# The second half of the first layer's w_in tiles serves two token groups at once

## The chip, the cores and the metric

The kernel runs on one core of one Trainium2 chip. The time is device microseconds (us) of one execution; of the kernel before three runs are known. About 0.5% is what a measurement of this kernel can tell from no change.

## The reference

Causal attention in blocks of 64 over 4 batches, 8 heads and 576 positions with 64 elements per head, then two feed-forward layers over all 2304 tokens, in float32:

```
scores = scale * q @ k.T; scores = where(block_i >= block_j, scores, -1e9)
x = softmax(scores) @ v                      # 2304 x 512 after the transpose of the heads
h = x @ w_in; x = (h - tanh(h)) @ w_out      # 512 -> 2048 -> 512
xn = x / sqrt(mean(x*x) + 1e-6) * rms_g
out = (silu(xn @ w_gate) * (xn @ w_val)) @ w_out2   # 512 -> 1536 -> 512
```

The change concerns the first feed-forward layer and the attention that is computed beside it.

## The kernel before

Every matrix product of the layers is made of three TensorE products: a float32 value is split into a rounded part (`h`, by the helper `rnd`, L88, mostly on ScalarE) and the rest (`l`, by `lo`, L94, a subtraction on VectorE or GpSimd), and the product is h*h + h*l + l*h. The page of the profile puts all of these splits down to L90 and L95.

The 2304 tokens are worked on in six groups of 384 (`NG`). The first layer has 16 tile steps (`J1`) in each group. A step `s` = (group g, tile j) has an in-product, L703 to L705 (12 matmuls 128x384, w_in tile j, into a PSUM tile `t`), then tanh on ScalarE (L711), `h - tanh(h)` on VectorE (L712, the kernel's "gelu" results), the split into `gh` and `gl`, and, one step later, the out-product of that tile, L619 to L621 (9 matmuls 128x512, w_out tile j, into three accumulators `acc`).

The weights of the first layer have to be brought into split form once. `stage1` loads a tile of 512 KB into `st` (L114), `convert` (L117 to L132) makes of it an h half and an l half with three ScalarE and four VectorE instructions (tiles `cv`, `cu`, `w1s`), and L584 writes the result to the DRAM tiles `w1d`. There are 32 tiles, w_in and w_out in turn. Seven of them (`EARLY`) are converted in the stretch before the first step, while the attention of group 0 runs; the other 25 during the 16 steps of group 0, which uses each as it is ready. Groups 1 to 5 load the tiles again from `w1d` (L590, 512 KB each, four buffers each of `w1s0` for w_in and `w1s1` for w_out).

Attention is cut into small steps (scores, transposes, product with v) in one list (`Attn.seq`), and TensorE's program order is written out by hand: `aslot` is called four times in a tile step and puts in as many attention steps as `upto` finds due. `goal(g)` says how far the list has to be by the end of group g: in group 0 to the end of group 1's attention (`end[1]`), in groups 1 to 4 a quarter of the rest each, and never less than the next group needs. Groups 0 and 1 have a lighter form of attention (plain float32, no split, scaling of the probabilities on GpSimd at L472). Group 5 has no attention beside it; there the second layer's weights are converted instead. The second layer (L782 to L822) follows. The order on VectorE, ScalarE, GpSimd and the SP queue is made by a scheduler; all DMAs are issued from SP.

Of the kernel before, what the change touches and what calls it, by code (L numbers as in the profile page):

```python
# [81 lines left out]
def build(ctx, tc, q, k, v, w_in, w_out, w_gate, w_val, w_out2, rms_g, ident_in, mask_in, out):  # L82
# [247 lines left out]
    class Attn:  # L330
# [222 lines left out]
    with tc.manual_schedule(engines={PE.engine}):  # L553
# [12 lines left out]
        for n in range(8):  # L566
            PE.matmul(warm, lhsT=zero[:, 0:128], rhs=zero[:, 0:512], start=True, stop=True)
        staged = {}
# [6 lines left out]
        w1t = {}  # L575

        def w1tile(n):
            return ring.tile([128, 1024], F32R, name=f"w1s{n % 2}", tag=f"w1s{n % 2}")

        def convert1(n):  # L580
# [4 lines left out]
            w1t[n] = (h, l)  # L585

        def w1load(n):
            t = w1tile(n)
            m = n % (2 * J1)
            SP.dma_start(out=t.bitcast(F32), in_=w1d[m])  # L590
            w1t[n] = (t[:, 0:512], t[:, 512:1024])
# [3 lines left out]
        def conv_upto(m):  # L595
            nonlocal ncv
            while ncv < min(m, 2 * J1):
                convert1(ncv)
                ncv += 1
                stage1(ncv + 2)  # L600
# [9 lines left out]

# [12 lines left out]
        def out1(s, t):  # L623
            g, j = divmod(s, J1)
            if j == 0:
                accs[t] = accp.tile([128, DM], F32, name=f"acc{t}", tag=f"acc{t}")
            gh, gl = gts[s]
            wh, wl = w1t[2 * s + 1]
            gemm_out(accs[t], gh, gl, wh, wl, t, j == 0, j == J1 - 1)
            if j == J1 - 1:  # L630
# [39 lines left out]

        NSA = NG * J1
        conv_upto(max(EARLY, 2))
        w2a = None
        nld = 2 * J1
        for s in range(NSA):
            g, j = divmod(s, J1)
            if j == 0:
                if g == 1:
                    st1.__exit__(None, None, None)
                    x4 = tc.tile_pool(name="x4", bufs=1, side="right")  # L680
                    env["x4"] = x4.__enter__()
                base, goal = att.pos, att.goal(g)
                nslots = 4 * J1 - 3
                si = 0

            def aslot():
                nonlocal si
                si += 1
# [157 lines left out]
```

## Time and profile before

| | us |
|---|---|
| median of three runs (lowest, highest) | 1127.95 (1122.27, 1128.41) |
| the profiled execution | 1128.99 |
| its span, first to last instruction | 1127.1 |
| start stretch, up to the first in-product | 57.5 |
| group 0 (16 steps) | 115.3 |
| group 1 | 103.9 |
| groups 2, 3, 4 | 102.6, 103.6, 101.9 |
| group 5 and the second layer | 542.3 |

The stretches are bounded by the first in-product of each group (57.5, 172.8, 276.7, 379.3, 482.9 and 584.8 us). Group 0 is also cut at the start of its tile 8 (109.6 us), and group 1 at its own (226.7 us). Matmuls are pipelined, so that two stand in the record at the same time and a busy TensorE is not TensorE at its peak; what a step really takes is read from the distance of its starts.

### The profile page before, as it was taken

To read this page: it belongs to the slowest core of one execution; us is meant where nothing else is said; L and a number is where in the kernel's file an instruction comes from. 1 tells how busy PE (TensorE), PEld (TensorE's weight loads), DVE (VectorE), ACT (ScalarE), POOL (GpSimd) and SP (SyncE) were. 2 spreads that over 40 slices of the span, in tenths; PEclk is the share of its full clock that TensorE was granted. 3 is DMA by queue.
4 is the path that set the end of the run, shared out by engine and by line. 5 is a ranking of instruction groups with operands and counts; after the bars stand their busy time and mean duration, and the time that the engine had idled before them with its cause. 6 is when DMAs were issued, how large, how long until landed. Compare 5 with 4: busy or idle time off the path is not lost.

```text
span 1127.1 us, 17140 instructions
## 1 busy us (share of the span) xinstructions
PE 1089.7 (97%) x5852; PEld 956.5 (85%) x5852; DVE 689.7 (61%) x1536; ACT 580.8 (52%) x1351; POOL 205.1 (18%) x286
## 2 busy tenths in 40 slices
PE   9899889999999999999999999899999999999998
PEld 6477668888888888788888989799999999999997
DVE  6789887887888878888757878822222222222212
ACT  6677777766777676666656686611112211121111
POOL 2534421343334242424210000000000000000000
PEclk9899999999999999999999999999999999999999
DMA  7799889778988887787569955400000000000000
GB/s 177 210 274 281 263 274 301 199 207 214 236 215 211 235 224 204 190 236 197 182 196 395 363 165 170 140 29 19 10 28 19 30 19 19 29 10 1 29 1 29
DMA packets 215496, 175.64 MB, mean 156 GB/s; under 512 B 159472, under 2 KB 180208, under 8 KB 215408
## 3 DMA queue, kind: packets, MB, share of 16 engines
q1 hardware_dynamic: 215408, 174.54, 53.8%
q8 instruction: 47, 0.77, 0.3%
q14 instruction: 41, 0.34, 0.1%
HBM read 148.28 MB, written 26.21 MB: 155 GB/s over the span
## 4 chain that ended last, share of the span: by engine, by line
PE 62%; DVE 12%; DMA 11%; ACT 7%; issue 3%; SPq 1%; POOL 1%; DVEq 0%; ACTq 0%; POOLq 0%
PE gv L798 8%; PE gv L796 8%; PE gv L797 7%; PE acc L619 7%; PE acc L621 7%; PE acc L620 7%; PE t L703 4%; DMA st<-in_moe_w_out 3%; PE t L705 3%; PE t L704 3%; PE t L436 3%; PE t L488 2%; DMA st<-in_moe_w_val 2%; DVE pt L472 2%; DVE pt L455 2%
## 5 line engine op out<-in xcount | busy, mean ns | idle before, releaser
L796 PE MATMUL gv<-xh,w_h 128*128 128x384 f32 x576 | 195.3, 339 | 2.6 <-ACT w_h L90 2.6
L798 PE MATMUL gv<-xh,w_l 128*128 128x384 f32 x576 | 194.2, 337 | 1.2 <-DVE w_l L95 1.0
L797 PE MATMUL gv<-xl,w_h 128*128 128x384 f32 x576 | 193.4, 336 | 0.0
L806 DVE TENSOR_TENSOR gt<-gv,gt 128x384 f32<-128x384 f32 x72 | 40.0, 556 | 236.0 <-PE gv L798 236.0
L90 ACT ACTIVATE gh<-gt 128x384 fp32r<-128x384 f32 x168 | 87.5, 521 | 152.5 <-DVE gt L806 137.1
L703 PE MATMUL t<-xh,w1s 128*128 128x384 f32 x384 | 140.7, 366 | 7.0 <-ACT w1s L90 5.7
L705 PE MATMUL t<-xh,w1s 128*128 128x384 f32 x384 | 131.2, 342 | 2.5 <-DVE w1s L95 2.4
L458 ACT ACTIVATE pt<-pt,stat 128x128 f32<-128x128 f32 (+3 forms) x160 | 96.1, 601 | 72.2 <-DVE pt L455 70.9
L704 PE MATMUL t<-xl,w1s 128*128 128x384 f32 x384 | 130.3, 339 | 0.0
L619 PE MATMUL acc<-w1s,gh 128*128 128x512 f32 x288 | 123.5, 429 | 3.3 <-ACT x2s L90 1.7
L805 ACT ACTIVATE gt<-gv 128x384 f32<-128x384 f32 x72 | 35.3, 490 | 162.5 <-PE gv L798 162.5
L95 DVE TENSOR_TENSOR gl<-gt,gh 128x384 fp32r<-128x384 f32 x152 | 92.0, 605 | 43.4 <-ACT gh L90 42.9
L621 PE MATMUL acc<-w1s,gl 128*128 128x512 f32 x288 | 114.9, 399 | 3.1 <-POOL gl L95 3.0
L796 PEld LDWEIGHTS gv<-xh,w_h 128*128 128x128 f32 x576 | 108.5, 188 | 6.5 <-ACT w_h L90 4.1
L620 PE MATMUL acc<-w1s,gh 128*128 128x512 f32 x288 | 113.8, 395 | 0.0
L798 PEld LDWEIGHTS gv<-xh,w_l 128*128 128x128 f32 x576 | 108.5, 188 | 2.5 <-DVE w_l L95 2.5
L797 PEld LDWEIGHTS gv<-xl,w_h 128*128 128x128 f32 x576 | 108.6, 189 | 2.4
L621 PE MATMUL acc<-w_h,gl 128*128 128x512 f32 x216 | 85.6, 396 | 0.6 <-DVE gl L95 0.6
L455 DVE TENSOR_SCALAR_CACHE_REDUCE pt<-t 128x128 f32<-128x128 f32 (+3 forms) x160 | 75.6, 473 | 16.4 <-PE t L439 11.1
L620 PE MATMUL acc<-w_l,gh 128*128 128x512 f32 x216 | 85.4, 395 | 0.0
L619 PE MATMUL acc<-w_h,gh 128*128 128x512 f32 x216 | 84.3, 390 | 0.4 <-ACT gh L90 0.4
L703 PEld LDWEIGHTS t<-xh,w1s 128*128 128x128 f32 x384 | 73.4, 191 | 12.2 <-ACT w1s L90 6.6
(101 smaller groups left out, 2140.7 us busy)
## 6 DMA issues: line engine op xcount, KB each, us to landing
w1s<-w1d SPq DMA_DIRECT2D x160, 512.0 KB, 4.6
w1d<-w1s SPq DMA_DIRECT2D x32, 512.0 KB, 5.3
st<-in_moe_w_out SPq DMA_DIRECT2D x28, 512.0 KB, 5.0
st<-in_moe_w_in SPq DMA_DIRECT2D x16, 512.0 KB, 5.3
st<-in_moe_w_gate SPq DMA_DIRECT2D x12, 512.0 KB, 3.9
st<-in_moe_w_val SPq DMA_DIRECT2D x12, 512.0 KB, 5.0
kr<-in_k SPq DMA_DIRECT2D x64, 72.0 KB, 4.2
x2d<-x2s SPq DMA_DIRECT2D x18, 256.0 KB, 3.7
```

Of the source, the lines that this page charges most:

```text
L95: eng.tensor_tensor(out=o, in0=full, in1=hi.bitcast(F32), op=ALU.subtract)
L455: DVE.tensor_scalar(pt[p0:128, a:z], s[p0:128, 0:z - a], -0.125, least, ALU.mult, ALU.min, accum_out=mx[n])
L458: ACT.activation(out=pt[p0:128, 0:keys], in_=pt[p0:128, 0:keys], func=AF.Exp, scale=-1.0, bias=least, accum_out=sm)
L619: PE.matmul(acc, lhsT=gh[:, c], rhs=wh, start=first, stop=False)
L620: PE.matmul(acc, lhsT=gh[:, c], rhs=wl, start=False, stop=False)
L621: PE.matmul(acc, lhsT=gl[:, c], rhs=wh, start=False, stop=last)
L703: PE.matmul(h, lhsT=wh[:, c], rhs=xh[:, kk], start=(kk == 0), stop=False)
L704: PE.matmul(h, lhsT=wh[:, c], rhs=xl[:, kk], start=False, stop=False)
L705: PE.matmul(h, lhsT=wl[:, c], rhs=xh[:, kk], start=False, stop=(kk == KD - 1))
L796: PE.matmul(ps, lhsT=wh[:, c], rhs=xh[:, kk], start=(kk == 0), stop=False)
L797: PE.matmul(ps, lhsT=wh[:, c], rhs=xl[:, kk], start=False, stop=False)
L798: PE.matmul(ps, lhsT=wl[:, c], rhs=xh[:, kk], start=False, stop=(kk == KD - 1))
```

## The change

Group 0's tiles 0 to 7 stay as they were. From tile 8 on, when a w_in tile has been converted, the in-product is made for group 0 and then for group 1 from the same tile. Group 1's results of these eight tiles are kept as one float32 tile each (`hs8` to `hs15`, in a new pool `half`). In the eight steps that follow, group 1 makes its in-products of tiles 0 to 7; each such step has two out-products, that of tile i-1 and that of tile 8+i-1, and `split` makes `sgh` and `sgl` of a kept tile first (one buffer of each). Two out-products of group 1 stand in the first step of group 2. Group 1 so loads no w_in tile of the second half again: 152 loads from `w1d` instead of 160.

The work is written as a list `steps` of (stretch, in-products, out-products), and the attention goals are a table by stretch: stretch 0 (tiles 0 to 7) has to reach the end of group 1's attention, stretch 1 (tiles 8 to 15, two in-products each) 6% of the rest, stretch 2 (group 1's last eight steps) 25%, then 48%, 74% and 100%. Group 2's attention output gets tiles of its own in `half`. Loads of `w1s` tiles are issued when a buffer is free, in the order of use.

```diff
     def xt(kind, n):
-            pool = env["x4"] if (kind, n) == ("A", B) else wk
+            pool = env[f"x{n}"] if kind == "A" and n in (2, B) else wk
...
-        def goal(self, g):
-
-            if g == 0 or g >= NG - 1:
-                return self.end[min(g + 1, NG - 1)]
+        def goal(self, g, share):
+
             c0, c1 = self.cost[self.end[1]], self.cost[-1]
-            even = next(m for m, c in enumerate(self.cost) if c >= c0 + (c1 - c0) * g / (NG - 2))
-            return max(self.end[g + 1], even)
+            even = next(m for m, c in enumerate(self.cost) if c >= c0 + (c1 - c0) * share)
+            return max(self.end[g], even)
...
+        JH = J1 // 2
+        steps = [(0 if j < JH else 1, [(0, j)] + [(1, j)] * (j >= JH), [(0, j - 1)] if j else [])
+                 for j in range(J1)]
+        steps += [(2, [(1, i)], [(1, i - 1), (1, JH - 1 + i)] if i else [(0, J1 - 1)]) for i in range(JH)]
+        for g in range(2, NG):
+            steps += [(g + 1, [(g, j)], [(g, j - 1)] if j else [(g - 1, J1 - 1)]) for j in range(J1)]
+        steps[J1 + JH][2].insert(0, (1, JH - 1))
+        steps.append((NG + 1, [], [(NG - 1, J1 - 1)]))
...
+        def w1ahead():
+            while ncv == 2 * J1:
+                xs_ = [x for x in range(2) if got[x] < len(uses[x]) and got[x] - done[x] < 4]
+                if not xs_:
+                    return
+                x = min(xs_, key=lambda x: uses[x][got[x]])
+                n = uses[x][got[x]][1]
+                SP.dma_start(out=w1tile(n).bitcast(F32), in_=w1d[n])
...
+        half = sa.enter_context(tc.tile_pool(name="half", bufs=1, side="left"))
+        env["x2"] = half
...
             ACT.activation(out=gt, in_=h, func=AF.Tanh)
+            if g == 1 and j >= JH:
+                hs = half.tile([128, TG], F32, name=f"hs{j}")
+                DVE.tensor_tensor(hs, h, gt, ALU.subtract)
+                gts[g, j] = hs
+                return
...
+        def split(g, j):
+            hs = gts[g, j]
+            gh = half.tile([128, TG], F32R, name="sgh", tag="sgh")
+            gl = half.tile([128, TG], F32R, name="sgl", tag="sgl")
+            rnd(ACT, gh, hs)
+            lo(DVE, gl, hs, gh)
+            gts[g, j] = (gh, gl)
...
+        goals = [(1, 0.0), (1, 0.06), (2, 0.25), (3, 0.48), (4, 0.74), (5, 1.0), (5, 1.0), (5, 1.0)]
...
+                stretch, base, goal = w, att.pos, att.goal(*goals[w])
+                nslots = sum(2 * len(i) + bool(i) + len(o) for w_, i, o in steps if w_ == w) - 3
...
+            w1ahead()
+            for g, j in outs:
+                if not isinstance(gts[g, j], tuple):
+                    split(g, j)
+            for g, j in ins:
+                in1(g, j)
+            if ins:
+                w1done(2 * ins[0][1])
+                aslot()
+            for g, j in outs:
+                out1(g, j, 0)
```

On TensorE, this is the end of an in-product of group 0 in tile 14 of the kernel before; `t` is the PSUM tile, `xh_421` group 0's tokens, `w1s0` the w_in tile, `pt` attention's probabilities:

```order
L704 MATMUL t_1958<-xl_422,w1s0_1827 128x384
L705 MATMUL t_1958<-xh_421,w1s0_1827 128x384
L619 MATMUL acc0_906<-w1s1_1757,gh_1922 128x512
L620 MATMUL acc0_906<-w1s1_1757,gh_1922 128x512
L621 MATMUL acc0_906<-w1s1_1757,gl_1923 128x512
L619 MATMUL acc1_920<-w1s1_1757,gh_1922 128x512
L620 MATMUL acc1_920<-w1s1_1757,gh_1922 128x512
L621 MATMUL acc1_920<-w1s1_1757,gl_1923 128x512
L619 MATMUL acc2_924<-w1s1_1757,gh_1922 128x512
L620 MATMUL acc2_924<-w1s1_1757,gh_1922 128x512
```

The out-product of the tile before follows it at once. In the changed kernel the same in-product of group 0 is followed by a second one, for group 1's tokens (`xh_949`, `xl_950`), of the same w_in tile:

```order
L716 MATMUL t_2233<-xl_422,w1s0_2019 128x384
L717 MATMUL t_2233<-xh_421,w1s0_2019 128x384
L434 MATMUL t_2259<-kp_1762,qh_1775 128x256
L434 MATMUL t_2259<-kp_1762,ql_1777 128x256
L437 LDWEIGHTS mkb_97
L437 MATMUL t_2259<-mkb_97 128x64
L715 MATMUL t_2258<-xh_949,w1s0_2019 128x384
L716 MATMUL t_2258<-xl_950,w1s0_2019 128x384
L717 MATMUL t_2258<-xh_949,w1s0_2019 128x384
```

The out-product of group 0 comes after both, so that it stands 12 matmuls later than before.

On ScalarE, these are the rows around the second in-product of group 1 in the kernel before; L711 is tanh, `gh` the rounded part, `pt`, `pp`, `qh` and `avt` belong to attention:

```order
L90 ACTIVATE gh_2171<-gt_2168 128x384
L90 ACTIVATE pp_2193<-t_2217 128x2x128
L458 ACTIVATE pt_2190,stat_2189<-pt_2190,stat_2189 128x256
L90 ACTIVATE qh_2340<-qt_2338 128x384
L458 ACTIVATE pt_2190,stat_2189<-pt_2190,stat_2189 128x384
L711 ACTIVATE gt_2245<-t_2210 128x384
L466 ACTIVATE stat_2189<-stat_2189 128x3
L90 ACTIVATE avt_2259<-t_2252 64x384
L90 ACTIVATE vp_2283<-vr_2034 128x6x64
L90 ACTIVATE gh_2248<-gt_2245 128x384
```

In the changed kernel the rounding of a kept tile (`sgh` from `hs9`) stands between the rounding of group 1's new tile and the next tanh (L723):

```order
L90 ACTIVATE gh_2581<-gt_2578 128x384
L464 ACTIVATE stat_2510<-stat_2510 128x3
L90 ACTIVATE sgh_2654<-hs9_1812 128x384
L456 ACTIVATE pt_2638,stat_2637<-pt_2638,stat_2637 128x512
L90 ACTIVATE pp_2659<-t_2660 128x128
L90 ACTIVATE qh_2798<-qt_2796 128x192
L90 ACTIVATE pp_2659<-t_2684 128x2x128
L723 ACTIVATE gt_2695<-t_2658 128x384
```

It writes the only buffer of `sgh`, so it waits until TensorE has read the kept tile before it, and tanh stands five rows behind it.

On the SP queue, where the last conversions end, the kernel before issues the first loads for group 1 so (`w1d_0_64` is w_in tile 0, `w1d_1_65` w_out tile 0, L584 the write of a converted tile, `vr` a load for attention):

```order
L584 DMA w1d_29_93<-w1s1_1757 128x1024
L590 DMA w1s0_1897<-w1d_0_64 128x1024
L590 DMA w1s0_1954<-w1d_2_66 128x1024
L590 DMA w1s0_1996<-w1d_4_68 128x1024
L274 DMA vr_2034<-in_v 128x3x64
L584 DMA w1d_30_94<-w1s0_1827 128x1024
L274 DMA vr_2034<-in_v 128x3x64
L590 DMA w1s1_1899<-w1d_1_65 128x1024
L590 DMA w1s1_1956<-w1d_3_67 128x1024
L584 DMA w1d_31_95<-w1s1_1849 128x1024
```

The changed kernel issues the load of w_out tile 8 (`w1d_17_81`) as the second load into `w1s1`, where w_out tile 1 stood:

```order
L627 DMA w1d_28_92<-w1s0_2019 128x1024
L627 DMA w1d_29_93<-w1s1_2045 128x1024
L613 DMA w1s0_2227<-w1d_0_64 128x1024
L613 DMA w1s0_2231<-w1d_2_66 128x1024
L613 DMA w1s0_2316<-w1d_4_68 128x1024
L627 DMA w1d_30_94<-w1s0_2111 128x1024
L613 DMA w1s1_2229<-w1d_1_65 128x1024
L613 DMA w1s1_2314<-w1d_17_81 128x1024
```

From here on two w_out tiles and one w_in tile are loaded for each step of stretch 2.

## Rows read from the trace of the kernel before

**Rows 1.** The stretches: span, busy us of each engine (instructions), granted clock, DMA share, GB/s.

```profile
core 0: us, PE busy (x) PEld busy (x) DVE busy (x) ACT busy (x) POOL busy (x), PEclk, DMA share, GB/s
0.00:57.50 57.50, 49.21 (x245) 31.05 (x246) 39.68 (x131) 39.85 (x122) 22.70 (x44) 0.91 0.76 194
57.50:109.60 52.10, 49.20 (x245) 37.87 (x244) 46.28 (x96) 41.01 (x100) 21.22 (x22) 1.00 0.96 282
109.60:172.80 63.20, 54.08 (x252) 42.79 (x251) 53.61 (x109) 44.66 (x107) 21.98 (x21) 0.92 0.90 272
172.80:226.70 53.90, 51.37 (x306) 45.24 (x306) 44.63 (x126) 40.23 (x113) 14.85 (x19) 1.00 0.86 243
226.70:276.70 50.00, 49.89 (x287) 43.38 (x286) 42.65 (x99) 32.82 (x78) 17.26 (x26) 1.00 0.84 209
276.70:379.30 102.60, 100.79 (x592) 88.78 (x592) 85.96 (x230) 75.08 (x199) 35.00 (x45) 1.00 0.86 222
379.30:482.90 103.60, 101.32 (x569) 86.97 (x569) 85.31 (x196) 67.91 (x159) 39.53 (x60) 1.00 0.80 210
482.90:584.80 101.90, 101.04 (x578) 87.98 (x578) 76.96 (x178) 64.39 (x150) 32.57 (x51) 1.00 0.67 196
```

**Rows 2.** The same columns, eight steps of group 5, without attention beside them.

```profile
584.80:618.30 33.50, 33.36 (x167) 29.67 (x166) 23.25 (x42) 21.54 (x41) 0.00 (x0) 1.00 1.03 381
```

**Rows 3.** Timeline, all engines: start, duration, instruction; the first in-product of group 1.

```profile
172.82 0.42 PE L703 MATMUL t<-xh,w1s 128*128 128x384 f32 x1
```

**Rows 4.** Waits of TensorE from 57.5 to 172.8 us: total us, times, longest us.

```profile
PE t L703 <- ACT w1s L90: 5.7, 4, 2.1
PE acc L621 <- POOL gl L95: 3.0, 5, 1.4
PE t L705 <- DVE w1s L95: 2.4, 3, 1.1
```

**Rows 5.** VectorE by shape, 57.5 to 172.8 us: busy us, mean ns, idle before and releaser.

```profile
L95 DVE TENSOR_TENSOR w1s<-cv,w1s 128x512 fp32r<-128x512 f32 x27 | 22.1, 819 | 4.7 <-ACT w1s L90 4.6
L130 DVE SCALAR_TENSOR_TENSOR cv<-st,cv 128x512 int32<-128x512 int32 x26 | 20.1, 773 | 0.2
L129 DVE SCALAR_TENSOR_TENSOR cv<-cv,cu 128x512 int32<-128x512 int32 x26 | 19.9, 767 | 0.5
L128 DVE TENSOR_SCALAR cv<-cv 128x512 f32<-128x512 f32 x26 | 14.4, 552 | 2.5 <-ACT cv L125 2.5
L712 DVE TENSOR_TENSOR gt<-t,gt 128x384 f32<-128x384 f32 x16 | 8.7, 547 | 0.4 <-ACT gt L711 0.4
```

**Rows 6.** VectorE by shape, 181 to 655 us, conversions of the second layer and gelu.

```profile
L712 DVE TENSOR_TENSOR gt<-t,gt 128x384 f32<-128x384 f32 x79 | 43.6, 552 | 22.0 <-ACT gt L711 21.1
L129 DVE SCALAR_TENSOR_TENSOR cv<-cv,cu 128x512 int32<-128x512 int32 x13 | 9.0, 692 | 1.3
L95 DVE TENSOR_TENSOR w_l<-cv,w_h 128x512 fp32r<-128x512 f32 x13 | 9.0, 690 | 2.4 <-ACT w_h L90 2.1
L130 DVE SCALAR_TENSOR_TENSOR cv<-st,cv 128x512 int32<-128x512 int32 x13 | 8.9, 686 | 0.1
L128 DVE TENSOR_SCALAR cv<-cv 128x512 f32<-128x512 f32 x14 | 5.9, 423 | 0.6 <-ACT cv L125 0.5
```

**Rows 7.** Timeline at 109 us, VectorE and GpSimd.

```profile
109.14 1.06 POOL L95 TENSOR_TENSOR gl<-gt,gh 128x384 fp32r<-128x384 f32 x1 [2.25 <-ACT gh L90]
109.24 1.24 DVE L128 TENSOR_SCALAR cv<-cv 128x512 f32<-128x512 f32 x1
```

**Rows 8.** Three stretches of group 0, columns as in rows 1.

```profile
133.50:136.80 3.30, 2.98 (x9) 2.98 (x10) 2.74 (x5) 2.24 (x5) 0.00 (x0) 0.50 0.81 197
157.30:160.70 3.40, 3.40 (x14) 3.11 (x13) 3.40 (x10) 1.85 (x4) 0.00 (x0) 0.51 0.81 205
167.60:171.00 3.40, 3.40 (x11) 3.12 (x10) 2.09 (x4) 1.31 (x3) 0.00 (x0) 0.50 0.92 304
```

**Rows 9.** The stretch 560 to 580 us, group 4, few loads for attention.

```profile
560.00:580.00 20.00, 20.00 (x117) 17.41 (x116) 14.15 (x29) 10.69 (x25) 5.84 (x7) 1.00 0.48 159
```

More of the change, by code (lines that the diff above doesn't have):

```diff
@@ L567, in build @@
             PE.matmul(warm, lhsT=zero[:, 0:128], rhs=zero[:, 0:512], start=True, stop=True)
+        JH = J1 // 2
[6 more added lines that the diff above has]
+        steps.append((NG + 1, [], [(NG - 1, J1 - 1)]))
+        outorder = {}
+        for _, _, outs in steps:
+            for g, j in outs:
+                outorder.setdefault(g, []).append(j)
         staged = {}
@@ L573, in stage1, with w1use, w1done @@
                 staged[n] = stage(rows_(w_out, j) if half else cols(w_in, j))
-        w1t = {}
-        def w1tile(n):
-            return ring.tile([128, 1024], F32R, name=f"w1s{n % 2}", tag=f"w1s{n % 2}")
+        uses = [[], []]
+        for st_n, (_, ins, outs) in enumerate(steps):
+            for g_, j_ in outs:
+                uses[1].append((st_n, 2 * j_ + 1))
+            for g_, j_ in ins:
+                if not uses[0] or uses[0][-1] != (st_n, 2 * j_):
+                    uses[0].append((st_n, 2 * j_))
+        got, done = [0, 0], [0, 0]
+        live = {}
+        def w1tile(n):
+            x = n % 2
+            t = ring.tile([128, 1024], F32R, name=f"w1s{x}", tag=f"w1s{x}")
+            assert uses[x][got[x]][1] == n and got[x] - done[x] < 4
+            live[x, got[x]] = (t[:, 0:512], t[:, 512:1024])
+            got[x] += 1
+            return t
+        def w1ahead():
[6 more added lines that the diff above has]
+                SP.dma_start(out=w1tile(n).bitcast(F32), in_=w1d[n])
+        def w1use(n):
+            assert uses[n % 2][done[n % 2]][1] == n
+            return live[n % 2, done[n % 2]]
+        def w1done(n):
+            live.pop((n % 2, done[n % 2]))
+            done[n % 2] += 1
         def convert1(n):
@@ L596, in conv_upto @@
             nonlocal ncv
-            while ncv < min(m, 2 * J1):
+            while ncv < min(m, 2 * J1) and got[ncv % 2] - done[ncv % 2] < 4:
                 convert1(ncv)
@@ L669, in w2_piece, with in1 @@
             convert(st, *w2[j][part])
[L671 to L688, printed above, removed]
[L689 to L697 removed]
+        def in1(g, j):
+            xh, xl = xt("A", g)
             h = env["t"].tile([128, 512], F32, name="t", tag="t")[:, 0:TG]
[L699 removed]
+            wh, wl = w1use(2 * j)
             aslot()
@@ L739, in build @@
                     env["ev"] = sev.enter_context(tc.tile_pool(name="ev", bufs=3, side="right"))
-            if g == NG - 1:
+            if w == NG:
+                j = ins[0][1]
                 if j == 5:
@@ L748, in build @@
                     w2_piece(j, w2a)
-        for t in range(TT):
-            out1(NSA - 1, t)
         rms(15, 18)
```

61 lines of the change are left out of this document (31 added, 30 removed).

## The prediction

> **What bounds the kernel now.** I read the stretches first. [rows 1] show two kinds. In the start stretch and in group 0 the record of TensorE has gaps (49.2 of 57.5, 49.2 of 52.1 and 54.1 of 63.2 us), while VectorE is busy 39.7, 46.3 and 53.6 us and the DMA engines 0.76, 0.96 and 0.90 of the time. From 172.8 us on TensorE's record is closed but for 0.1 to 2.5 us a stretch, and VectorE is busy 76 to 85% of the time. So group 0 is led by the conversions, groups 1 to 4 by TensorE with VectorE close behind.
>
> The second view is a stretch where TensorE does nothing but the layer: eight steps of group 5 take 33.5 us [rows 2], 4.19 us a step. The in-product and the out-product have the same number of columns (12 x 384 and 9 x 512), so each is put at 2.09 us. Sixteen steps are 67.0 us, group 0 takes 115.3. The starts of the groups are read from the timeline, as 172.8 us for group 1 [rows 3].
>
> The third view is what TensorE waits for in group 0: the converted tile's h half 5.7 us, its l half 2.4, GpSimd's `gl` 3.0 [rows 4]. That is 11 of the 115.3 - 103.3 = 12 us that its record is open; the rest of the loss is slower running. In three stretches of about 3.4 us, all behind 109.6 us, its granted clock was 0.50, the lower of its two levels (1.2 GHz) [rows 8]. At half clock 3.4 us give 1.7 us of work, so the three cost TensorE 5.1 us at most. Before tile 8 the clock was 1.00 [rows 1].
>
> **The change part by part.** The sum is made against the profiled execution (1128.99 us, 1.0 above the median of 1127.95) and over groups 0 and 1, 57.5 to 276.7 us, 219.2 us. Behind them the attention list stands where it stood (25% of the rest), and the shares of groups 2 to 4 (23, 26, 26 instead of 25%) add up to the same.
>
> *What moves.* 8 x 12 in-product matmuls, 16.7 us of TensorE, go from group 1 into the second half of group 0. Group 1's attention, spread over 16 steps, must end in 8. Nothing is computed twice: VectorE has 364 instructions in groups 0 and 1 before and 361 after, counted in the program's order between the first steps and the first step of group 2; the three missing stand before the first step, like three of ScalarE. I put 1.0 us on the start stretch for them (three conversions at 0.55 to 0.82 us [rows 5] beside a ScalarE and VectorE that are each busy 69% [rows 1]; between 0 and 2.2).
>
> *Stretch 0 (tiles 0 to 7).* VectorE has 110 instructions instead of 82: 43 of conversions (47 before), 8 gelu subtractions, 59 of attention (27 before). A conversion's instruction costs 0.73 us on average [rows 5], one of attention about 0.44: group 1's first half has 101 instructions in 44.6 us [rows 1]. So 46.3 - 4 x 0.73 + 32 x 0.44 = 57.5 us busy. Before, these steps took 52.1 us for 46.3, a factor of 1.126; with it stretch 0 takes **64.7 us**. Bounds: 1.00, a VectorE that is never idle, gives 57.5, and 1.179, the second half's factor, 67.8. For the range I go down to 1.05 (60.4), since no stretch with conversions came near 1.00. TensorE is not later here: 15 half-steps are 31.4 us, and all that its record holds in group 0 beyond the layer is 103.3 - 67.0 = 36.3 us, in sum 67.7 if every bit of that moved here. DMA: a pair of loads for attention is priced by group 2, 0.86 x 102.6 = 88.2 us of transfers less 32 tiles; a tile is 1.53 us (share 0.48 [rows 9] at two tiles per step of 101.9 / 16 = 6.4 us), so 39.2 us are left for six pairs, 6.5 each. The order brings at most two more pairs ahead of tile 8 and takes one conversion (two transfers) out: 50.0 + 13.1 - 3.1 = 60.0 us, a share of 0.93 in 64.7. It fits, barely.
>
> *Stretch 1 (tiles 8 to 15, two in-products).* 121 VectorE instructions instead of 100: 53 of conversions (51), 16 subtractions (8, at 0.547 us [rows 5]), 51 of attention (41), one more. 53.6 + 1.5 + 4.4 + 4.8 = 64.3 us busy. The factor was 63.2 / 53.6 = 1.179; with the half-clock stretches gone wholly it is 58.1 / 53.6 = 1.084. TensorE has 24 half-steps (50.2 us) and 6% of the rest of attention, 8.6 us, so its gaps shrink and the low clock should mostly go, but both engines are then above 80% and wait for each other. I take 1.10: **70.7 us**; bounds 1.05 and 1.179, 67.5 to 75.8.
>
> *Stretch 2 (group 1's last eight steps).* TensorE: 8 in-products and 15 out-products, 48.1 us. Attention at the price of groups 2 to 4: 308.1 us less 48 x 4.19 = 201.1 leaves 107.0 for 75%, 1.43 us per percent, with all small gaps in it; 19% are 27.1. **75.2 us.** VectorE has 130 instructions at 0.48 (87.3 us for 182 in group 1), 62 us, and hides. Bounds: VectorE at its factor of 1.126 would need 70, the least that can be; with each `sgh` late by 0.5 us it is 79. The split of a kept tile waits on ScalarE for the last read of the one before, with five rows ahead of tanh behind it; it is asked for an in-product (2.09 us) and an out-product later, so I put it at nothing, and 0.5 us each, 4 us, if that cover is gone.
>
> *Group 2* starts with one out-product more, 2.1 us. *Eight loads less* are 12.2 us of transfers in a stretch whose DMA share was 0.84 to 0.86: nothing, since no wait of TensorE there is for a transfer. Group 2's own tiles for attention's output remove a reuse that no wait in the profile shows.
>
> Sum: 1.0 + 64.7 + 70.7 + 75.2 + 2.1 = 213.7 against 219.2, **-5.5 us**, 1123.5 us.
>
> *A rule beside it.* A conversion's first VectorE instruction takes 0.55 us in group 0 and 0.42 later, the others 0.77 to 0.82 and 0.69, while the subtraction L712, which has one operand in PSUM, stays at 0.55 [rows 5, 6]. At 109.24 us the first took 1.24 us and ended behind a GpSimd subtraction that ran to 110.20 [rows 7]. Two operands in SBUF beside GpSimd are slow here, and stretch 0 brings GpSimd 31 instructions instead of 22, stretch 1 16 instead of 21, at 1.0 us each (43.2 us for 43 [rows 1]). The Trainium skill (SBUF — State Buffer, Who interferes with whom) calls this an exclusive lock: an instruction with two SBUF inputs blocks on a reading GpSimd one until it ends. The trace agrees, at 1.24 against 0.42 us. By the rows the conversions of group 0 are 11 us slower beside 43 us of GpSimd, 0.26 per us: 2.3 us more in stretch 0, 1.3 less in stretch 1. With it the sum would be -4.5, without it -5.5; I leave it out, since it is smaller than what the factors leave open.
>
> **The rivals.** *Nothing gained.* The conversions keep their pace: stretch 1 at 1.179 is 75.8 us, the sum -0.4, 1128.6 us. For it: [rows 4] shows TensorE waiting for converted tiles, and there are as many after; SP's one queue was at 0.90. Against: the half-clock stretches lie just there. *More gained.* TensorE, fed all the time, keeps its clock, and stretches 0 and 1 come to 1.05: 60.4 + 67.5 + 75.2 + 3.1 = 206.2, -13.0, 1116.0 us. For it: VectorE's idle time in 57.5 to 276.7 us is 32 us. Against: both stretches with conversions were at 1.126 or above. *Slower.* Group 1's attention is a chain (scores, maximum, exponential, scaling on GpSimd, transposes, product), and in 8 steps its latency is no longer covered. In the start stretch, where group 0's eight heads ran in a like time, VectorE was busy only 39.7 of 57.5 us, 69%. At that share stretch 0 takes 57.5 / 0.69 = 83.3 us, 18.6 more, 1142.1 us. It decides from the point where VectorE's share in stretch 0 falls below 0.75 (76.7 us: +6.5, 1135.5). Against: the start stretch has load latency at its front and TensorE empty; in group 0 the scheduler found 89%. *The change doesn't do what it says:* if group 1's attention ended late, the first in-products of tile 8 would wait and the second products of stretch 1 with them; the order has them in place, so this is part of the slower case.
>
> **How the numbers follow.** Forecast (a gain of 3 to 9 us) 0.46, nothing gained (-3 to +5) 0.26, more gained 0.15, slower 0.13. 0.5% is 5.6 us. The forecast lies on that line: 0.29 of its 0.46 is put beyond it, since the factors' lower ends are farther away than the upper ones, and with the case of more gain and a little of the spread of the case of none that is 0.46 faster; 0.40 the same; 0.14 slower. The range is 1114 (just under the case of more gain) to 1133 (stretches 0 and 1 at 1.179 and stretch 2 at 79: 67.8 + 75.8 + 79 + 3.1 = 225.7, +6.5, less a little); the forecast's own is 1119 to 1127.
>
> **What would show it.** Right: stretch 0 of 62 to 68 us with VectorE at 0.87 or more; stretch 1 of 67 to 74 us with a granted clock of 1.00; stretch 2 of 72 to 78 us with TensorE's record closed; the three together shorter than 219.2 by 5 to 9; group 2 longer by 2. Wrong: TensorE waiting over 8 us for converted tiles in stretch 1, waits for `pt` or `pp` of attention at the end of stretch 0, `sgh` or `sgl` among the waits of stretch 2, or group 2 to 4 moving by more than 3 us.

## The result, and the profile after

The changed kernel takes 1134.19 us (median of 8 runs, 1130.59 to 1138.51), the kernel before 1128.09 beside it (8 runs, 1122.27 to 1130.27). The ratio is 1.0058, 95% interval 1.0033 to 1.0084: slower, by 6.1 us, where 5.5 us less were forecast. It lies just outside the range. The profiled execution took 1130.59 us (span 1128.2) and was the fastest of its eight, while the one before was 0.9 us above its median. So the two profiles show only 1.1 us of the 6.1.

These are the stretches of the changed kernel, in the columns of [rows 1]: the start, stretches 0, 1 and 2, and groups 2, 3 and 4.

```profile
core 0: us, PE busy (x) PEld busy (x) DVE busy (x) ACT busy (x) POOL busy (x), PEclk, DMA share, GB/s
0.00:55.30 55.30, 45.70 (x248) 28.56 (x249) 39.12 (x131) 40.28 (x124) 22.77 (x44) 0.97 0.79 202
55.30:122.60 67.30, 62.11 (x321) 47.37 (x319) 57.91 (x139) 54.26 (x146) 28.68 (x33) 0.97 0.83 231
122.60:193.10 70.50, 63.25 (x337) 57.43 (x335) 63.23 (x133) 49.55 (x113) 19.24 (x16) 0.95 0.81 264
193.10:268.50 75.40, 74.38 (x419) 62.91 (x417) 62.33 (x159) 54.52 (x138) 25.18 (x37) 1.00 0.88 225
268.50:374.50 106.00, 103.62 (x603) 90.69 (x601) 86.25 (x227) 73.98 (x198) 35.01 (x45) 1.00 0.85 216
374.50:478.70 104.20, 100.87 (x566) 86.64 (x565) 87.42 (x193) 66.89 (x157) 38.55 (x58) 1.00 0.78 211
478.70:587.10 108.40, 103.39 (x582) 88.39 (x581) 82.66 (x180) 64.37 (x153) 33.97 (x53) 1.00 0.62 183
```

Read against [rows 1]: groups 0 and 1 end at 268.5 instead of 276.7 us, 8.2 us earlier, and at the end of group 2 the changed kernel is still 4.8 us ahead (374.5 against 379.3). Then group 4 takes 108.4 instead of 101.9 us. TensorE does much the same there (582 and 578 matmuls recorded), but VectorE, with two instructions more, is busy 82.7 instead of 77.0 us. The lead is gone where no step of the forecast looked.

What TensorE waits for in the changed kernel (total us, times, longest), first in stretch 1, then in group 4:

```profile
PE t L717 <- DVE w1s L95: 7.1, 4, 3.1
...
PE t L434 <- DVE pp L95: 2.7, 3, 1.3
PE acc L656 <- DVE x2s L92: 1.1, 1, 1.1
PE t L513 <- DVE pp L95: 1.1, 1, 1.1
```

Group 4 waits 4.9 us for VectorE; before it waited 0.9. Of the 4.9 us, 1.1 are for `x2s`, a copy that VectorE itself could start only after an earlier store of it had landed; the other 3.8 are for `pp`, a subtraction that empties a PSUM tile. VectorE's instructions that got longer there are above all the softmax scalings, L470 (L472 in the kernel before). By shape, over group 4 of the changed kernel (busy us, mean ns):

```profile
L470 DVE TENSOR_SCALAR pt<-pt,stat 64x576 f32<-64x576 f32 x10 | 8.3, 834 | 0.1
L470 DVE TENSOR_SCALAR pt<-pt,stat 128x512 f32<-128x512 f32 x10 | 7.8, 778 | 0.2
```

and over group 4 of the run with equal shares (below), where the group is as short as before:

```profile
L470 DVE TENSOR_SCALAR pt<-pt,stat 64x576 f32<-64x576 f32 x10 | 6.4, 642 | 0.1
L470 DVE TENSOR_SCALAR pt<-pt,stat 128x512 f32<-128x512 f32 x10 | 5.2, 518 | 0.1
```

Twenty instructions of the same shapes take 16.1 instead of 11.6 us. One place of the changed kernel's timeline (start, duration, instruction) shows why, and who pays:

```profile
544.85 1.57 POOL L95 TENSOR_TENSOR vp<-vr,vp 128x640 fp32r<-128x640 f32 x1 [2.32 <-ACT stat L464]
545.04 1.66 DVE L470 TENSOR_SCALAR pt<-pt,stat 128x512 f32<-128x512 f32 x1
...
546.50 0.65 POOL L517 TENSOR_TENSOR xs<-avt 64x192 f32<-64x192 f32 x1
...
546.72 0.75 DVE L470 TENSOR_SCALAR pt<-pt,stat 64x576 f32<-64x576 f32 x1
...
547.50 0.49 DVE L95 TENSOR_TENSOR pp<-t,pp 128x320 fp32r<-128x320 f32 x1
...
548.05 0.40 PE L434 MATMUL t<-kp,qh 128*128 128x288 f32 x1 [1.12 <-DVE pp L95]
```

A GpSimd subtraction runs to 546.42. The first of the two scalings of a head begins while it runs. With no GpSimd instruction beside it, a scaling of 128x512 takes 0.44 to 0.49 us and one of 64x576 takes 0.52 us (groups 3 and 4 of the run with equal shares), 1.0 us for the pair. Here the first takes 1.66 us and ends 0.28 us behind the subtraction; the second begins beside the next GpSimd instruction, which runs to 547.15, takes 0.75 us and ends at 547.47. The pair takes 2.43 us instead of 1.0. Behind it in VectorE's order stands the subtraction for `pp` that empties a PSUM tile, and the next scores product waits 1.12 us for that tile.

This place is one of many. In group 4 of the changed kernel nine of the twenty scalings began with 0.25 us or more of a GpSimd instruction still to run, and each ended 0.28 to 0.32 us behind the end of that instruction, however far off that was; with equal shares three of twenty were held so. Scalings that a GpSimd instruction joined 0.15 us or more after their start took 0.47 to 0.52 us, as if alone. One pair shows both:

```profile
525.64 0.47 DVE L470 TENSOR_SCALAR pt<-pt,stat 128x512 f32<-128x512 f32 x1
525.89 1.64 POOL L95 TENSOR_TENSOR vp<-vr,vp 128x640 fp32r<-128x640 f32 x1 [2.89 <-DMA w1s<-w1d]
526.12 1.73 DVE L470 TENSOR_SCALAR pt<-pt,stat 64x576 f32<-64x576 f32 x1
```

The Trainium skill (SBUF — State Buffer, Who interferes with whom) says that `tensor_scalar` can enter a mode that takes the port pair shared with GpSimd, and that the later of the two then blocks fully; these rows agree, at 1.73 us for the scaling that came later and 0.47 for the one that came first.

At this place the scalings are 1.4 us longer than alone, more than the 1.12 us that TensorE waits. At the two other long waits for `pp` (1.34 us before 538.1, 1.08 us before 573.1) the pair ahead of the subtraction took 1.39 and 1.46 us, only 0.4 to 0.5 us longer than alone. So part of the loss is the place of the pair ahead of `pp`, and not its length.

### The profile page after: what moved, and what is told of

The parts are those of the page before. It is cut to its first block, busy times and chain, and to the rows that moved or that the text cites. A ratio compares the mean times of both kernels' runs of the same rounds, so it can differ in the third digit from the quotient of the medians.

```text
span 1128.2 us, 17127 instructions
## 1 busy us (share of the span) xinstructions
PE 1084.2 (96%) x5852; PEld 952.9 (84%) x5852; DVE 693.1 (61%) x1536; ACT 578.8 (51%) x1351; POOL 203.4 (18%) x286
## 4 chain that ended last, share of the span: by engine, by line
PE 60%; DVE 14%; DMA 11%; ACT 7%; issue 3%; SPq 2%; POOL 1%; DVEq 0%; ACTq 0%; POOLq 0%
PE gv L852 8%; PE gv L850 7%; PE gv L851 7%; PE acc L656 7%; PE acc L658 7%; PE acc L657 7%; PE t L715 3%; PE t L717 3%; DMA st<-in_moe_w_out 3%; PE t L716 3%; DVE pt L470 2%; PE t L434 2%; DVE pt L453 2%; PE t L486 2%; DMA qr<-in_q 2%
## 5 line engine op out<-in xcount | busy, mean ns | idle before, releaser
L90 ACT ACTIVATE gh<-gt 128x384 fp32r<-128x384 f32 x160 | 83.3, 521 | 150.4 <-DVE gt L860 135.7
L859 ACT ACTIVATE gt<-gv 128x384 f32<-128x384 f32 x72 | 35.3, 490 | 162.3 <-PE gv L852 162.3
L656 PE MATMUL acc<-w1s,gh 128*128 128x512 f32 x264 | 112.4, 426 | 2.7 <-DMA xin<-x2d 1.2
L95 DVE TENSOR_TENSOR gl<-gt,gh 128x384 fp32r<-128x384 f32 x144 | 83.3, 579 | 38.7 <-ACT gh L90 38.1
L658 PE MATMUL acc<-w1s,gl 128*128 128x512 f32 x264 | 104.8, 397 | 1.5 <-DVE gl L95 1.5
L657 PE MATMUL acc<-w1s,gh 128*128 128x512 f32 x264 | 104.2, 395 | 0.0
L434 PE MATMUL t<-kp,qh 128*128 128x288 f32 (+4 forms) x240 | 76.7, 357 | 10.2 <-DVE pp L95 6.2
```

Source lines behind the costliest of these rows:

```text
L434: PE.matmul(s[:, 0:z - a], lhsT=x[:, c0:c0 + 128], rhs=y[:, a:z], start=(n == 0), stop=(n == len(parts) - 1 and not last))
L656: PE.matmul(acc, lhsT=gh[:, c], rhs=wh, start=first, stop=False)
L657: PE.matmul(acc, lhsT=gh[:, c], rhs=wl, start=False, stop=False)
L658: PE.matmul(acc, lhsT=gl[:, c], rhs=wh, start=False, stop=last)
```

## The experiments

"Groups" are read from each run's own profile, which is one execution. A ratio is to runs of the kernel before in the same session; the sessions are the first four experiments, then four, four, four and the last two. Two ratios of different sessions are compared by these ratios alone.

**The changed kernel, and the kernel before, once more.** No edit.

> The changed kernel once more, for a second profile. In the first one groups 0 and 1 were 6.0 us shorter than before (213.2 against 219.2), group 2 3.4 longer, group 4 6.5 longer, and the start stretch 2.2 and the start of the second layer 1.9 shorter, both where the kernel before had a half-clock stretch. Theory A (the gain of groups 0 and 1 is real and is given back in groups 2 and 4, the rest is where half-clock stretches happen to fall): groups 2 and 4 are again 105 to 107 and 107 to 109.5 us, groups 0 and 1 together 211 to 216, the time 1132 to 1137. Rival B (the profile was a lucky run, and most runs lose the 6 us in groups 0 and 1 to a lower clock): groups 0 and 1 at 217 to 222 with more half-clock stretches, groups 2 and 4 as before.

1130.47 us against 1123.88: 1.0068 (1.0039 to 1.0097). Groups 0 and 1 together 212.3, group 2 106.6, group 4 107.9 us. The loss and its place come again: theory A, with the time 1.5 us below its bounds.

> The kernel before once more, for a second profile. Theory A: groups 2, 3 and 4 at 102 to 104 us each again, groups 0 and 1 at 217 to 221. Rival B: groups 0 and 1 move by several us from run to run with the half-clock stretches (three in the first profile).

One run, 1125.55 us. Groups 0 and 1 take 216.2 us here and 219.2 in the profile that the forecast worked from, with one half-clock stretch instead of three in group 0; groups 2 to 4 agree within 0.4 us. Three later runs have the same instructions in the same order up to the end of group 1 (the kernel before with 0.74, and twice with the scalings on GpSimd): 218.6, 218.9 and 218.4 us. So one profile of these groups can be 3 us off, and the mean of the five, 218.2, says that the base of the sum was some 1 us high.

**Sharing undone, in the changed kernel's code.**

```
-        steps = [(0 if j < JH else 1, [(0, j)] + [(1, j)] * (j >= JH), [(0, j - 1)] if j else [])
-                 for j in range(J1)]
-        steps += [(2, [(1, i)], [(1, i - 1), (1, JH - 1 + i)] if i else [(0, J1 - 1)]) for i in range(JH)]
+        steps = [(0, [(0, j)], [(0, j - 1)] if j else []) for j in range(J1)]
+        steps += [(2, [(1, j)], [(1, j - 1)] if j else [(0, J1 - 1)]) for j in range(J1)]
...
-        goals = [(1, 0.0), (1, 0.06), (2, 0.25), (3, 0.48), (4, 0.74), (5, 1.0), (5, 1.0), (5, 1.0)]
+        goals = [(1, 0.0), (1, 0.0), (2, 0.25), (3, 0.5), (4, 0.75), (5, 1.0), (5, 1.0), (5, 1.0)]
```

> The changed code with one in-product per tile in group 0 and 16 steps of group 1 as before, attention goals as before (end of group 1, 25, 50, 75, 100%); the new loader and group 2's own tiles stay. Theory A: as before, 1126 to 1130 us, ratio to before 0.998 to 1.002, since the loss comes with the sharing and its shares. Rival C (the loader, which issues up to four w_in and four w_out tiles ahead on the one SP queue, or the new tiles cost the time): 3 to 6 us slower than before, with groups 2 and 4 longer.

1.0056 (1.0037 to 1.0075). Groups 0 and 1 take 224.1 us (in an execution 2.2 us above the median), but group 4 is back at 101.7. So sharing is not what lengthens group 4, and the code without sharing is itself no copy of the kernel before: it costs about as much, in another place. Rival C had the time about right and the place wrong.

**Only the shares.**

```
-        goals = [(1, 0.0), (1, 0.06), (2, 0.25), (3, 0.48), (4, 0.74), (5, 1.0), (5, 1.0), (5, 1.0)]
+        goals = [(1, 0.0), (1, 0.06), (2, 0.25), (3, 0.5), (4, 0.75), (5, 1.0), (5, 1.0), (5, 1.0)]
```

> The changed kernel with 50 and 75% in place of 48 and 74%, so that groups 3 and 4 have the same share of attention and, in VectorE's order, the same place of the scalings as before (in 4 of 23 cases a subtraction for pp stands right behind two scalings in group 4, in the changed kernel in 6 of 24). Theory A: group 4 at 101 to 103 us instead of 108.4, group 3 at 103 to 104, group 2 about 3 us longer than in the changed kernel (109); the time 3 to 5 us below the changed kernel's, 1129 to 1131. Rival B or C: the time stays at 1133 to 1135.

1122.79 us, 0.9992 (0.9975 to 1.0009); from the means of the runs, 8.6 us (5.6 to 11.5) less than the changed kernel beside it. Group 4 is 101.7 us. 0.5 for 0.48 gives the same program, since group 2 has to reach the end of group 3's own attention, at 51% of the rest; 0.75 for 0.74 is all that changed, two of the 384 steps of the attention list. Theory A for group 4, but the time fell by about twice what it said.

**The same one percent in the kernel before.**

```
-            even = next(m for m, c in enumerate(self.cost) if c >= c0 + (c1 - c0) * g / (NG - 2))
+            even = next(m for m, c in enumerate(self.cost) if c >= c0 + (c1 - c0) * (0.74 if g == 3 else g / (NG - 2)))
```

> The kernel before with one number changed: attention has to reach 74% in place of 75% at the end of group 3. No sharing, the old loader. Theory A2 (the loss of the changed kernel is the 0.74 alone: it moves attention's steps against group 4's tile steps, and VectorE's order then puts two scalings ahead of the subtraction that frees a PSUM tile in 6 of 24 cases instead of 4 of 23): group 4 at 107 to 109 us instead of 101.8, group 3 within 1 us, the time 5 to 7 us above before, ratio 1.004 to 1.007. Rival D (the loss in group 4 comes from what the sharing leaves behind, or the loader's order): group 4 at 102 to 103.5, 1% of the rest of attention, the time within 0.2% of before.

1.0056 (1.0036 to 1.0076). Group 4 takes 107.0 us, and its twenty scalings 16.1 us, as in the changed kernel. One entry of the share table costs what the whole change costs, with no sharing in the program.

**The scalings of the last 12 of 32 pairs on GpSimd.**

```
-                (POOL if u.light else DVE).tensor_scalar(pv, pv, sc, 1.0, ALU.mult, ALU.mult)
+                (POOL if u.light or i >= 20 else DVE).tensor_scalar(pv, pv, sc, 1.0, ALU.mult, ALU.mult)
```

> The changed kernel (0.74) with the scalings of the last twelve pairs, which run beside groups 3 and 4, on GpSimd instead of VectorE. Theory A2 (TensorE waits in group 4 for subtractions that stand behind VectorE's scalings): group 4 falls from 108 to 102 to 104 us, the waits of TensorE for pp go. Rival E (group 4 is long because of the order of attention and tile steps on TensorE itself, or because VectorE is full): group 4 stays at 107 or more, or moves with GpSimd's waits for pt.

1119.01 us, 0.9951 (0.9932 to 0.9971), with 0.74 still in place. Groups 3 and 4 (same columns):

```profile
373.60:472.90 99.30, 99.30 (x567) 86.74 (x566) 69.17 (x171) 68.39 (x158) 54.65 (x83) 1.00 0.81 221
472.90:575.70 102.80, 101.52 (x580) 88.44 (x581) 64.00 (x159) 64.72 (x152) 47.61 (x73) 1.00 0.64 194
```

TensorE's record is closed in group 3, and VectorE has 69.2 instead of 87.4 us of work there. Theory A2; that group 3 falls too, from 104.2 to 99.3 us, it did not say.

**Equal shares, and group 2 with one attention slot less** (its extra out-product brings one slot more than groups 3 and 4 have).

```
-                nslots = sum(2 * len(i) + bool(i) + len(o) for w_, i, o in steps if w_ == w) - 3
+                nslots = sum(2 * len(i) + bool(i) + len(o) for w_, i, o in steps if w_ == w) - 3 - (w == 3)
...
-                aslot()
+                if w != 3 or (g, j) == outs[-1]:
+                    aslot()
```

> The changed kernel with 75% as in the run with equal shares, and with the first step of group 2 without an extra place for attention at its second out-product, so that attention stands against group 2's tile steps as before. Theory A2 (phase): group 2 falls from 106.7 to 104 to 105 us (102.4 before plus one out-product of 2.1), the time 1120 to 1122.5, below before by 0.2 to 0.4%. Rival: group 2's length is the out-product and work left over from stretch 2, and stays at 106 to 107.

0.9983 (0.9966 to 1.0000); group 2 takes 104.2 us instead of 106.7, groups 0 and 1 together 214.3 instead of 211.1. No difference in time from equal shares alone (measured in another session).

**Sharing undone, with the attention slots of the kernel before**, so that TensorE's order is the same row for row. To the edit of the run with sharing undone comes:

```
-                nslots = sum(2 * len(i) + bool(i) + len(o) for w_, i, o in steps if w_ == w) - 3
+                nslots = sum(2 * len(i) + bool(i) + len(o) for w_, i, o in steps if w_ == w) - 3 + (w == 0)
```

> Sharing undone again, now with 61 places for attention in group 0, so that TensorE's order is that of before in every instruction; loader and group 2's own tiles stay, and the orders of SP, VectorE and ScalarE differ in group 0 and 1. If the 6 us of the first such run were attention's places in group 0: within 0.2% of before. If they are the loader and the order it brings: again 0.4 to 0.7% slower, in groups 0 and 1.

1.0046 (1.0031 to 1.0060), with groups 3 and 4 at 103.6 and 101.7 us as in the kernel before, and group 2 at 104.5 with a half-clock stretch in it. What is left of the loss is in what else the change brought, the loader with the order that it gives the other engines, or group 2's own tiles, since TensorE's work and its order are those of the kernel before.

**The same, with loads no further ahead than before.**

```
-                xs_ = [x for x in range(2) if got[x] < len(uses[x]) and got[x] - done[x] < 4]
+                xs_ = [x for x in range(2) if got[x] < len(uses[x]) and got[x] - done[x] < 3 + x]
```

> The changed kernel with the sharing undone and the attention slots of the kernel before, as in the experiment before, and now also with the loads of first-layer tiles no further ahead than in the kernel before: three w_in tiles and four w_out tiles ahead of the step instead of four and four. TensorE's order is that of the kernel before. Theory A (the loads that run one w_in tile further ahead displace attention's loads and cost the 0.46% that this base showed): it comes back to the kernel before, ratio 0.998 to 1.002, group 2 at 102 to 103 us instead of 104.5, groups 0 and 1 together at 216 to 219. Theory B (the other order of VectorE's and ScalarE's rows costs it): the ratio stays at 1.003 to 1.006.

1.0031 (1.0014 to 1.0048), on the edge of theory B. Taking the limit of four converted tiles (`got - done < 4` in `conv_upto`) away as well gives the order of the kernel before on every engine, so that limit and the place of group 2's own tiles for attention's output are all that is left to cost 0.3%; no run has both changes. The profile of this run has the groups of the kernel before (115.1, 103.9, 102.7, 103.6, 101.7 us), but it is of an execution 2.4 us below the median, so where the 0.3% lies it does not show.

**The scalings on GpSimd in the kernel before**, the same edit without the change.

> The kernel before, and only the softmax scalings of the last 12 of the 32 pairs on GpSimd instead of VectorE. Theory A (those scalings cost only where the order puts them ahead of a copy that TensorE waits for, which the changed kernel's share of 0.74 does in group 4 and the kernel before hardly does): groups 3 and 4 stay within 1 us of 103.6 and 101.9, ratio 0.997 to 1.001. Theory B (the scalings load VectorE everywhere, and the sharing has no part in what was gained by moving them): groups 3 and 4 shorten by 3 us or more together, ratio 0.990 to 0.995.

1119.36 us, 0.9954 (0.9933 to 0.9975). My theory A was wrong: group 3 falls from 103.6 to 99.9 us in the kernel before too. The scalings cost in group 3 as well, not only at 0.74. One rival is that any relief of VectorE helps. Against it stand three groups that lose all their scalings: where these took 0.58 us each on average (group 4 with 0.75) the group gains 0.9 us, where they took 0.72 (group 3 before) 3.7 us, and where they took 0.81 (group 4 with 0.74) 5.6 us. The gain goes with how long the scalings were held, not with their number (20, 22 and 20).

**Both: equal shares and the scalings on GpSimd; then also the shorter lookahead of loads.**

> The changed kernel with shares of 0.50 and 0.75 and the scalings of the last 12 pairs on GpSimd. Theory A (both edits remove the same waits of group 4): groups 3 and 4 together at 201 to 204 us, no better than with the scalings alone, ratio 0.993 to 0.997. Theory B (they add): group 3 at 99, group 4 at 100 to 101, ratio 0.988 to 0.992.

1119.56 us, 0.9955 (0.9932 to 0.9978): theory A by the ratio, though groups 3 and 4, at 99.9 and 100.8 us, are as short as B had them. With the scalings off VectorE, 0.74 (0.9951, in another session) and 0.75 cost the same as far as the intervals tell, though groups 3 and 4 together still take 1.4 us more with 0.74 (102.8 and 99.3 us); with the scalings on VectorE the ratios are 1.0068 and 0.9992.

> The same as the run before it (equal shares, scalings of the last 12 pairs on GpSimd), with the loads of w_in tiles three instead of four tiles ahead. If the longer lookahead costs what the base without sharing showed (0.46%), this is faster than the run before it by 3 to 5 us, ratio about 0.990; if it does not, the two agree within 0.2%, and group 2 stays at 104 to 107 us.

0.9940 (0.9921 to 0.9960), 0.5 us from the run above by the medians: the lookahead costs nothing that these runs can tell.

**0.76 and 0.73.** Is it the amount of attention in group 4, or where its steps fall?

> The changed kernel with shares of 0.50 and 0.76 instead of 0.48 and 0.74: 1% of the attention list moves from group 4 to group 3, against the 0.75 of the run with equal shares (groups 3 and 4: 103.6 and 101.7 us). Theory A (amount: a percent of the list costs 1.4 us where it stands): group 3 at 105.0, group 4 at 100.3, time as with equal shares, ratio 0.998 to 1.001. Theory B (where the steps fall: VectorE's order has the subtraction for a copy of pp straight behind two scalings in 7 of 23 cases in group 3 and 8 of 22 in group 4, against 4 of 22 and 4 of 23 with 0.75): groups 3 and 4 together 4 us or more longer, ratio 1.003 to 1.008.

1.0042 (1.0022 to 1.0062). Groups 3 and 4 with 0.76:

```profile
371.70:476.40 104.70, 102.56 (x576) 87.80 (x575) 89.64 (x198) 69.08 (x163) 44.43 (x64) 1.00 0.75 208
476.40:580.20 103.80, 101.87 (x571) 86.71 (x570) 79.54 (x176) 62.44 (x147) 30.69 (x49) 1.00 0.63 195
```

> The changed kernel with shares of 0.48 and 0.73 instead of 0.48 and 0.74: one more percent of the attention list goes from group 3 to group 4. Theory A (amount): group 4 gets longer by 1.4 us still, to 109.7, group 3 shorter, ratio 1.006 to 1.010. Theory B (where the steps fall: the subtraction for pp stands straight behind two scalings in 6 of 20 cases in group 3 and in 4 of 25 in group 4, against 6 of 21 and 6 of 24 with 0.74): group 4 comes back to 102 to 105 us, ratio 0.998 to 1.003.

1.0048 (1.0027 to 1.0070). Groups 3 and 4 with 0.73:

```profile
373.80:476.80 103.00, 100.20 (x553) 84.92 (x551) 83.74 (x181) 63.52 (x149) 39.28 (x57) 1.00 0.75 210
476.80:582.90 106.10, 104.72 (x593) 89.09 (x593) 85.85 (x193) 68.05 (x161) 37.74 (x55) 1.00 0.62 192
```

Groups 3 and 4 together take 208.5 and 209.1 us; with 0.75 they take 205.3, and with 0.74 212.6. Less attention in group 4 costs as well as more, so it is not the amount. Theory B, a count of rows that stand behind two scalings, had the ratio of 0.76 right (the sum of the two groups rose by 3.2 us, not by 4 or more), but not that of 0.73, which it put nearly back at 0.75.

The records of the two groups, added up, show what goes with the time. With 0.75, 0.76, 0.73 and 0.74 VectorE is busy 162.3, 169.2, 169.6 and 170.1 us in them for the same 373 instructions, the scalings 27.4, 32.3, 31.6 and 32.4 us of it; they run 11.0, 20.5, 19.3 and 18.5 us beside a busy GpSimd. So each of the three other shares makes VectorE's work 7 to 8 us longer. How much of that TensorE pays differs: its waits are 2.9, 3.5, 3.8 and 8.3 us, in the order of the times. 0.74 costs most with the least overlap of the three, so the overlap alone does not give the price; what stands behind the held instructions has a part in it.

**No limit on converted tiles ahead**, with equal shares.

```
-            while ncv < min(m, 2 * J1) and got[ncv % 2] - done[ncv % 2] < 4:
+            while ncv < min(m, 2 * J1):
```

> The changed kernel with equal shares, and without the limit of four converted tiles ahead of their use (the ring of four buffers alone decides, as in the kernel before). TensorE's order stays, VectorE's and ScalarE's in groups 0 and 1 change. Theory A (the limit costs what it cost without sharing, 0.3%, because conversions are issued later): 3 us faster than with equal shares, ratio 0.994 to 0.997, stretches 0 and 1 together at 130 to 134 us instead of 135 to 139. Theory B (the cost without sharing came from the granted clock's chance): ratio 0.997 to 1.001, stretches 0 and 1 at 135 to 139.

0.9981 (0.9961 to 1.0001). The wait of stretch 1 for `w1s` (7.1 us in the changed kernel) is gone, but stretches 0 and 1 still take 135.4 us: stretch 0 takes 73.1 us instead of 66.0. Theory B, as far as this interval tells.

> Equal shares, no limit on converted tiles ahead, and the scalings of the last 12 pairs on GpSimd. If the three gains add: ratio 0.990 to 0.993, and this is faster than the kernel before with the scalings alone (0.9954). If the sharing brings nothing beside the scalings: 0.994 to 0.997.

1114.90 us in four runs, 0.9916 (0.9882 to 0.9949). It was run again beside the kernel before with the scalings alone:

> Again equal shares, no limit on converted tiles ahead, scalings of the last 12 pairs on GpSimd, beside the run that follows. Theory A (the sharing is worth what its stretches show: groups 0 and 1 shorter by 4 to 6 us, group 2 longer by 4): 1.0 to 3.5 us faster than the kernel before with the scalings alone, ratio to the kernel before 0.991 to 0.995. Theory B (the sharing is worth nothing): the two within 1.0 us of one another.

> Again the kernel before with the scalings of the last 12 pairs on GpSimd, beside the run before: 0.9954 as measured already (0.993 to 0.998), whichever theory of the sharing holds.

1116.14 us, 0.9923 (0.9902 to 0.9944), and 1119.55, 0.9944 (0.9921 to 0.9967). From the means of the runs, sharing is 3.5 us faster (0.7 to 6.2): theory A, and the best version measured. The profile of the first is of the fastest of its six executions and that of the second of the slowest of its seven, so their stretches differ by more than the kernels do. Stretches 0 and 1 together, stretch 2, and groups 2 to 4 of it:

```profile
55.10:188.30 133.20, 120.86 (x653) 100.89 (x651) 123.92 (x271) 102.44 (x259) 47.98 (x48) 1.00 0.88 256
188.30:263.30 75.00, 74.06 (x420) 63.12 (x418) 62.73 (x159) 54.75 (x138) 25.16 (x39) 1.00 0.85 226
263.30:366.80 103.50, 102.89 (x601) 90.55 (x599) 82.21 (x222) 73.88 (x198) 38.20 (x50) 1.00 0.83 221
366.80:466.70 99.90, 99.90 (x568) 86.93 (x567) 70.05 (x173) 68.61 (x159) 55.89 (x84) 1.00 0.81 218
466.70:567.50 100.80, 100.80 (x578) 87.96 (x578) 63.86 (x157) 64.70 (x150) 47.17 (x71) 1.00 0.65 199
```

and the same groups of the kernel before with the scalings on GpSimd (group 0, group 1, groups 2 to 4):

```profile
59.20:172.10 112.90, 101.01 (x495) 79.09 (x493) 100.36 (x204) 85.79 (x205) 43.27 (x42) 0.97 0.93 278
172.10:277.50 105.40, 102.77 (x590) 89.92 (x589) 88.06 (x225) 73.13 (x191) 32.41 (x45) 0.98 0.81 230
277.50:378.70 101.20, 100.55 (x593) 88.76 (x592) 82.72 (x222) 75.10 (x199) 38.83 (x50) 1.00 0.84 223
378.70:478.60 99.90, 99.90 (x568) 86.92 (x567) 70.36 (x174) 68.59 (x159) 55.31 (x84) 1.00 0.80 218
478.60:579.40 100.80, 100.80 (x578) 87.98 (x578) 63.74 (x157) 64.91 (x150) 47.27 (x71) 1.00 0.65 198
```

Groups 3 and 4 are now the same to 0.1 us. What sharing is worth stands in the first two rows, 218.3 against 208.2 us, of which a part is the clock (1.00 throughout here, 0.97 and 0.98 there), less 2.3 us in group 2.

## Why the prediction was wrong, step by step

- *Start, 1.0 us more:* 2.2 less in the profile, but starts of 55.3 to 59.2 us were measured for one and the same order before the first step, so nothing of it is shown.
- *Stretch 0, 64.7:* 67.3, near the upper bound of 67.8. VectorE was busy 57.9 us, as worked out (57.5); its factor was 1.16, not 1.126. The share is 0.86, above the 0.75 from which the slower rival decides, so that rival did not decide, though the time came out near its 1135.5: that is luck. The waits it named came in small: 5.1 us for `pp` and `pt` of attention, 2.3 of them in the last 12 us of the stretch, which it had named as a sign of being wrong.
- *Stretch 1, 70.7:* 70.5. The waits for converted tiles were 7.1 us, just under the 8 that would have spoken against it. The granted clock did not go to 1.00 (0.95).
- *Stretch 2, 75.2:* 75.4, TensorE's record closed but for 1.0 us, no wait for `sgh` or `sgl`.
- *The three:* 213.2 against 219.2, 6.0 us shorter, where 8.6 were forecast (64.7 + 70.7 + 75.2 = 210.6). One profile each is not enough here. Nine profiles with the changed kernel's order in groups 0 and 1 give 210.5 to 214.6, mean 212.9; against the mean of 218.2 for the order before that is 5.3 shorter. So sharing shortens these groups, by less than two thirds of the forecast, and the term that was too good is mainly stretch 0 (mean 66.8).
- *Group 2, 2.1 longer:* 3.4. The extra out-product is there (603 matmuls for 592); 1.3 us more were not foreseen, and group 2 took 103.4 to 107.0 us in the shared runs. More than 3 us here or in group 4 was one of the signs of being wrong that the prediction had named.
- **The failing step:** "the shares of groups 2 to 4 (23, 26, 26 instead of 25%) add up to the same". They add up in work, not in time. (The shares themselves were misread: 0.48 has no effect, as the run with equal shares shows, and only the 0.74 moved anything, two steps of the list from group 3 to group 4.) The 0.74 in place of 0.75 cost 5 to 7 us of group 4: put into the kernel before it makes 1.0056, taken out of the changed kernel 1.0068 becomes 0.9992, and with the scalings moved to GpSimd it costs nothing that the ratios can tell (0.9951 and 0.9955). At the forecast's own price, 1.43 us per percent, the work that moved, 0.8% of the list, is worth 1.1 us. Why it costs more is read from the rows: nine instead of three scalings of group 4 are held by GpSimd's preparations, the twenty take 4.5 us longer, and TensorE waits 4.0 us more, 2.9 of them for `pp`, whose subtraction stands behind scalings at each of the three long waits. The prediction had the contention in its hands, [rows 7], and weighed it for the conversions of group 0 alone. The instruction of [rows 7] is a `tensor_scalar` with one input in SBUF, as the scalings are, and not the case of two inputs in SBUF that the prediction set beside it.
- *Even without that step* the forecast would have been too good: equal shares give 0.9992, the rival of nothing gained, because groups 0 and 1 gained 5.3 us instead of 8.6 and group 2 gave back 4.1 instead of 2.1. The loader may take some 3 us too: without sharing 0.31% of loss is left (1.0014 to 1.0048), and sharing paid in the version without the limit (3.5 us) and not in the one with it (0.9955 beside 0.9954). That the limit is the cause is not shown; with equal shares alone, lifting it moved the time by less than the intervals.

Left open: how much of group 4's loss is the longer scalings and how much their place ahead of the `pp` subtraction, since the one edit that removes the first removes the second (an order with `pp` first and the scalings still on VectorE was not run); and why 0.75 falls well and 0.73, 0.74 and 0.76 do not.

## What to carry to other kernels

Where several engines run in fixed orders that were balanced once, moving 1% of one list against another is a change of its own: list it as a part, and look at which instructions will run side by side, not only at the sum of work. Price VectorE instructions by what GpSimd does at the same moment; the cheap test is to compare one shape's mean duration across groups, and the cheap cure was to give the colliding instruction to GpSimd itself. And take the base of a sum from several profiles where a stretch holds half-clock pieces, since five profiles of one order gave 216.2 to 219.2 us for the same two groups.

## What the hardware showed that was not expected

A scaling of 128x512 took 0.44 to 0.49 us alone and 1.66 us when it began 0.19 us into a GpSimd subtraction of 1.57 us: in that group nine scalings were held so, and each ended 0.28 to 0.32 us behind the GpSimd instruction. One that began first (0.25 us before a GpSimd subtraction, at 525.64 us of the changed kernel) took 0.47 us. In group 4 of the changed kernel 10.6 us of the scalings ran beside a busy GpSimd, against 3.3 with equal shares, and the twenty took 4.5 us longer; the overlap is in part that waiting itself, so the two are not cause and effect. On GpSimd the same scalings took about 0.69 us (128x512) and 0.75 us (64x576). Moving them there made GpSimd busier (39.5 to 55.3 us in group 3 of the kernel before) and VectorE 15 us idler, and the group 3.7 us shorter.
